# SwiGLU feed-forward: one weight load for both column parts of the down projection

## The chip, the cores and the metric

The kernel runs on one core of a Trainium2 chip (trn2). The metric is the device time of one execution in microseconds (us), lower is better. Times in the tables are medians of several executions; a profile shows one execution. In the profiles PE is the tensor engine, PEld its weight loads, DVE the vector engine, ACT the scalar engine and POOL GpSimd.

## The reference

```python
def reference(x, w_gate, w_up, w_down):      # x: 1 x 2048 x 640, bf16
    g = silu(x @ w_gate)                     # 640 x 1536
    u = x @ w_up                             # 640 x 1536
    return (g * u) @ w_down                  # 1536 x 640
```

## The kernel before

The tensor engine (PE) holds a block of 128 x 128 "weights" (the stationary operand, `lhsT`) and streams columns of the other operand (`rhs`) through it. One call of `nc.tensor.matmul` becomes two instructions: a weight load (LDWEIGHTS, engine PEld in the profile) and the matmul itself (MATMUL, engine PE). The program works on four blocks of 512 rows. In each, 24 gate and up tiles of 5 matmuls with 512 columns come first, then the down projection of four row tiles of 128 rows. The output has 640 columns, and the kernel splits each row tile into a part `po_a` of 512 columns and a part `po_b` of 128, two accumulators in PSUM, the memory that the matmuls write. Both are summed over the same twelve blocks `aT[:, kf, s0:s0+P]` as weights:

```python
for j in range(SUB):                                   # 4 row tiles in each of 4 blocks
    s0 = sb * S_BLK + j * P
    last = sb == NSB - 1 and j == SUB - 1
    po_a = psum.tile([P, DA], f32, tag="po_a", name="po_a")            # DA = 512
    for kf in range(KF):                                               # KF = 12
        nc.tensor.matmul(po_a[:], lhsT=aT[:, kf, s0 : s0 + P],
                         rhs=wd_sb[:, kf, 0:DA], start=(kf == 0), stop=(kf == KF - 1))
    po_b = psum.tile([P, D - DA], f32, tag="po_b", name="po_b")        # 128 columns
    for kf in range(KF):
        nc.tensor.matmul(po_b[:], lhsT=aT[:, kf, s0 : s0 + P],
                         rhs=wd_sb[:, kf, DA:D], start=(kf == 0), stop=(kf == KF - 1))
    ot = outp.tile([P, D], bf16)
    nc.scalar.copy(ot[:, 0:DA], po_a[:])
    # ... copy of po_b, output DMA
```

(The calls are set on fewer lines here; the loads of the inputs and the start are cut. `po_a` and `po_b` have two buffers each.) The second loop thus loads twelve weight blocks that the first loop has loaded shortly before.

## Time and profile before

| | before |
|---|---|
| time, median of the 4 runs compared with the change | 166.74 us (166.44 to 166.98) |
| span of the profiled execution | 165.2 us |
| matmuls / weight loads in the program | 907 / 907 |
| PE busy, PEld busy | 160.5 us, 80.3 us |
| matmul start to next start: 512 columns, 128 columns | 216 ns, 56 ns |
| one down projection stage (4 row tiles) | 13.04 us |

Lines of the page of the kernel before: the span, the busy times, the chain of work that ended last by engine and by line, and groups of instructions. In a group line the columns are: source line, engine, operation, out<-in, shapes, count, then busy us and mean ns of one record, then the idle time of the engine before them.

```profile
span 165.2 us, 2137 instructions
...
PE 160.5 (97%) x890; PEld 80.3 (49%) x907; DVE 34.9 (21%) x52; ACT 43.5 (26%) x81; POOL 0.7 (0%) x6
...
PE 97%; issue 1%; DVE 0%; ACT 0%
PE pg L112 31%; PE pu L112 31%; PE po_a L150 25%; PE po_b L159 7%; PE pw L98 2%; PE pt L105 1%; DVE xT L108 0%; ACT ot L173 0%
...
L150 PE MATMUL po_a<-wd_sb,aT 128*128 128x512 bf16 x185 | 43.4, 379 | 0.3
...
L150 PEld LDWEIGHTS <-aT 128*128 128x128 bf16 x192 | 18.3, 98 | 19.8
...
L159 PEld LDWEIGHTS <-aT 128*128 128x128 bf16 x192 | 12.1, 98 | 3.8
L159 PE MATMUL po_b<-wd_sb,aT 128*128 128x128 bf16 x192 | 13.3, 220 | 0.1
```

PE is busy for 97% and is 97% of the chain that ended last: no other engine or transfer holds it up. PEld is busy for 80.3 us, 30.4 us of it at the two lines of the down projection (L150 and L159). It has to be read with care, because records of PE and PEld overlap each other. A 512-column matmul is recorded with 379 ns and a 128-column matmul with 220 ns, and yet they follow each other much faster. The record of PE is incomplete too: 890 of its 907 matmuls are there, and each missing one looks like a short gap.

The timeline of the same kernel around a change from `po_a` to `po_b` (start us, duration us, then the group, merged):

```profile
start us, us, engine line op out<-in xcount [idle before <-releaser]
...
34.58 0.87 PEld L159 LDWEIGHTS <-aT 128*128 128x128 bf16 x12
34.80 0.83 PE L159 MATMUL po_b<-wd_sb,aT 128*128 128x128 bf16 x12
...
35.47 0.59 PE L150 MATMUL po_a<-wd_sb,aT 128*128 128x512 bf16 x2
```

Twelve `po_b` matmuls start at 34.80, and the next tile's `po_a` starts at 35.47: 0.67 us for twelve, 56 ns each. Twelve weight loads of about 98 ns lie in the same stretch, from 34.58 on. So the loads run beside the matmuls, also here, where the matmuls are shortest. In the single records a load starts 1 to 3 ns after the start of the matmul before it, 1 or 2 ns nearly everywhere (where it seems later, the record of a matmul is missing).

### The profile page before, as it was taken

The numbers are of one execution on the slowest core, as the hardware profiler recorded it, in microseconds if no ns is written. First come the engines' busy times: TensorE is split into PE (matmuls) and PEld (weight loads), VectorE is DVE, ScalarE is ACT, GpSimd is POOL, SyncE is SP. The second block draws the span as 40 slices with busy tenths as digits, with TensorE's granted clock in tenths as the row PEclk, the third lists the DMA queues.
The fourth block names the chain that finished last, engine by engine and source line by source line (L and its number), as shares of the span: only waits on it lengthen the run. The fifth ranks groups of instructions, "written<-read, shape, count | busy, mean of one in ns | idle before, by whom it ended". The sixth has DMA issues, their size and how long they took to land.

```text
span 165.2 us, 2137 instructions
## 1 busy us (share of the span) xinstructions
PE 160.5 (97%) x890; PEld 80.3 (49%) x907; DVE 34.9 (21%) x52; ACT 43.5 (26%) x81; POOL 0.7 (0%) x6
## 2 busy tenths in 40 slices
PE   8999999999999999999999999999999999999992
PEld 2844444455644444455554444445654444445551
DVE  0433333300013333310003333330002233331000
ACT  3042222222332222223232222222232222222222
POOL 1000000000000000000000000000000000000000
PEclk9999999999999999999999999999999999999999
DMA  5999999801110000001110000001111000000121
GB/s 147 294 326 327 362 230 223 160 29 55 40 40 0 0 4 0 0 0 42 68 55 0 0 2 0 0 4 40 40 40 40 4 0 0 0 0 0 46 78 40
DMA packets 18906, 11.27 MB, mean 68 GB/s; under 512 B 9681, under 2 KB 18897, under 8 KB 18897
## 3 DMA queue, kind: packets, MB, share of 16 engines
q1 hardware_dynamic: 18096, 10.95, 24.2%
q10 hardware_dynamic: 800, 0.20, 0.5%
q8 instruction: 7, 0.11, 0.3%
q14 instruction: 3, 0.02, 0.0%
HBM read 6.55 MB, written 2.62 MB: 56 GB/s over the span
## 4 chain that ended last, share of the span: by engine, by line
PE 97%; issue 1%; DVE 0%; ACT 0%
PE pg L112 31%; PE pu L112 31%; PE po_a L150 25%; PE po_b L159 7%; PE pw L98 2%; PE pt L105 1%; DVE xT L108 0%; ACT ot L173 0%
## 5 line engine op out<-in xcount | busy, mean ns | idle before, releaser
L112 PE MATMUL pg<-xT,wg_sb 128*128 128x512 bf16 (+2 forms) x244 | 59.5, 371 | 0.4
L112 PE MATMUL pu<-xT,wu_sb 128*128 128x512 bf16 (+2 forms) x241 | 59.6, 375 | 0.2
L141 DVE TENSOR_TENSOR aT<-sg,pu 128x512 bf16<-128x512 f32 x48 | 33.0, 687 | 109.2 <-PE pu L112 108.0
L140 ACT ACTIVATE sg<-pg 128x512 f32<-128x512 f32 x48 | 28.7, 597 | 76.2 <-PE pg L112 76.2
L150 PE MATMUL po_a<-wd_sb,aT 128*128 128x512 bf16 x185 | 43.4, 379 | 0.3
L112 PEld LDWEIGHTS <-wu_sb 128*128 128x128 bf16 x245 | 23.7, 98 | 27.9
L112 PEld LDWEIGHTS <-wg_sb 128*128 128x128 bf16 x250 | 24.0, 98 | 27.2 <-issue 0.2
L150 PEld LDWEIGHTS <-aT 128*128 128x128 bf16 x192 | 18.3, 98 | 19.8
L167 ACT CAST ot<-po_a 128x512 bf16<-128x512 f32 x16 | 9.4, 585 | 40.4 <-PE po_a L150 38.0
L159 PEld LDWEIGHTS <-aT 128*128 128x128 bf16 x192 | 12.1, 98 | 3.8
L159 PE MATMUL po_b<-wd_sb,aT 128*128 128x128 bf16 x192 | 13.3, 220 | 0.1
L98 PE MATMUL pw<-const-bfloat16-1.0 128*128 128x512 bf16 x8 | 3.6, 625 | 0.8 <-PEq L189 0.8
L169 ACT CAST ot<-po_b 128x128 bf16<-128x128 f32 x15 | 4.0, 265 | 1.1
L108 DVE COPY xT<-pt 128x640 bf16<-128x640 bf16 x4 | 2.0, 490 | 5.8 <-PE pt L105 5.7
L105 PEld LDWEIGHTS <-x_sb 128*128 128x128 bf16 x20 | 2.0, 133 | 0.6 <-DMA x_sb<-in_x_dram 0.5
L105 PE MATMUL pt<-ident,x_sb 128*128 128x128 bf16 x20 | 2.2, 289 | 0.0
L98 PEld LDWEIGHTS <-const-bfloat16-1.0 128*128 128x128 bf16 x8 | 1.0, 137 | 2.4 <-issue 2.4
L140 ACT ACT_TABLE_LOAD x1 | 1.3, 1283 | 1.3 <-PEq L189 1.3
masks.py:199 POOL TENSOR_SCALAR_AFFINE_SELECT ident<-ident 128x128 bf16<-128x128 bf16 x1 | 0.3, 292 | 0.1
L173 ACT CAST ot<-po_b 128x128 bf16<-128x128 f32 x1 | 0.3, 265 | 0.0
masks.py:197 POOL MEMSET ident<- 128x128 bf16 x1 | 0.2, 204 | 0.3 <-POOLq L189 0.3
L189 POOL MEMSET const-bfloat16-1.0<- 128x1 bf16 x1 | 0.1, 101 | 0.0
(3 smaller groups left out, 0.3 us busy)
## 6 DMA issues: line engine op xcount, KB each, us to landing
out_dram<-ot SPq DMA_DIRECT2D x15, 160.0 KB, 1.8
wd_sb<-in_w_down_dram SPq DMA_DIRECT2D x1, 1920.0 KB, 12.5
wg_sb<-in_w_gate_dram SPq DMA_DIRECT2D x3, 480.0 KB, 7.0
wu_sb<-in_w_up_dram SPq DMA_DIRECT2D x3, 480.0 KB, 7.6
x_sb<-in_x_dram SPq DMA_DIRECT2D x1, 320.0 KB, 3.2
x_sb<-in_x_dram SPq DMA_DIRECT2D x2, 160.0 KB, 3.7
wg_sb<-in_w_gate_dram SPq DMA_DIRECT2D x1, 320.0 KB, 5.0
wu_sb<-in_w_up_dram SPq DMA_DIRECT2D x1, 320.0 KB, 5.5
```

Of the source, the lines that this page charges most:

```text
L98: nc.tensor.matmul(pw[:], lhsT=ones[:, 0:P], rhs=ones, start=True, stop=True)
L105: nc.tensor.transpose(out=pt[:, kd, :], in_=x_sb[:, c, kd * P : (kd + 1) * P], identity=ident[:])
L108: nc.vector.tensor_copy(out=xT[:, :, c * P : (c + 1) * P], in_=pt[:])
L112: nc.tensor.matmul(ps[:, c0:c1], lhsT=w_sb[:, kd, fc * P : (fc + 1) * P], rhs=xT[:, kd, sb * S_BLK + c0 : sb * S_BLK + c1], start=(kd == 0 ...
L140: nc.scalar.activation(sg[:], pg[:], ACT.Silu)
L141: nc.vector.tensor_tensor(out=aT[:, fc, s_sl], in0=sg[:], in1=pu[:], op=ALU.mult)
L150: nc.tensor.matmul(po_a[:], lhsT=aT[:, kf, s0 : s0 + P], rhs=wd_sb[:, kf, 0:DA], start=(kf == 0), stop=(kf == KF - 1),)
L159: nc.tensor.matmul(po_b[:], lhsT=aT[:, kf, s0 : s0 + P], rhs=wd_sb[:, kf, DA:D], start=(kf == 0), stop=(kf == KF - 1),)
L167: nc.scalar.copy(ot[:, 0:DA], po_a[:])
L169: nc.scalar.copy(ot[:, DA:D], po_b[:])
L173: nc.scalar.copy(ot[:, DA:D], po_b[:])
L189: nc = _bacc.Bacc("TRN2", target_bir_lowering=False, num_devices=1)
```

## The change

Its intent is to load each weight block once and to stream both column parts past it. The loops are interleaved, and after compilation a pass over the instruction list deletes every weight load that loads what the engine already holds and that carries no semaphore. A semaphore is the signal by which one engine waits for another. The last row tile keeps its old order, so that the copy of `po_a` can run while `po_b` is still computed. (The diff is shortened: calls stand on one line, `down_mm` is the same matmul as a function, and the wrapper that calls `_share_weights` after `tc.compile()` is cut.)

```diff
-            for kf in range(KF):
-                nc.tensor.matmul(po_a[:], lhsT=aT[:, kf, s0 : s0 + P], rhs=wd_sb[:, kf, 0:DA], ...)
-            for kf in range(KF):
-                nc.tensor.matmul(po_b[:], lhsT=aT[:, kf, s0 : s0 + P], rhs=wd_sb[:, kf, DA:D], ...)
+            if last:
+                ...                                    # po_a, then po_b, as before
+            else:
+                for kf in range(KF):
+                    down_mm(po_a, 0, DA, kf)
+                    down_mm(po_b, DA, D, kf)
...
+def _share_weights(nc):
+    for block in nc.main_func.blocks:
+        held, drop = None, []
+        for k, ins in enumerate(block.instructions):
+            if ins.engine != mybir.EngineType.PE:
+                continue
+            if isinstance(ins, mybir.InstLdweights):
+                what = str(ins.ins[0])
+                s = ins.sync_info
+                free = s is None or not (s.on_wait or s.on_update)
+                if free and what == held:
+                    drop.append(k)
+                held = what
+        for k in reversed(drop):
+            del block.instructions[k]
```

187 loads go: 180 in the down projection (15 row tiles of 12) and 7 of the 8 of the warm-up matmuls at the start.

More of the change, by code (lines that the diff above doesn't have):

```diff
@@ L10, with _body @@
 @with_exitstack
-def kernel(
+def _body(
     ctx: ExitStack,
@@ L148, with down_mm @@
             po_a = psum.tile([P, DA], f32, tag="po_a", name="po_a")
-            for kf in range(KF):
+            po_b = psum.tile([P, D - DA], f32, tag="po_b", name="po_b")
+            def down_mm(po, d0, d1, kf):
                 nc.tensor.matmul(
-                    po_a[:],
+                    po[:],
                     lhsT=aT[:, kf, s0 : s0 + P],
-                    rhs=wd_sb[:, kf, 0:DA],
+                    rhs=wd_sb[:, kf, d0:d1],
                     start=(kf == 0),
@@ L156 @@
                 )
-            po_b = psum.tile([P, D - DA], f32, tag="po_b", name="po_b")
-            for kf in range(KF):
-                nc.tensor.matmul(
-                    po_b[:],
-                    lhsT=aT[:, kf, s0 : s0 + P],
-                    rhs=wd_sb[:, kf, DA:D],
-                    start=(kf == 0),
-                    stop=(kf == KF - 1),
-                )
+            if last:
+                for kf in range(KF):
+                    down_mm(po_a, 0, DA, kf)
+                for kf in range(KF):
+                    down_mm(po_b, DA, D, kf)
+            else:
+                for kf in range(KF):
+                    down_mm(po_a, 0, DA, kf)
+                    down_mm(po_b, DA, D, kf)
             ot = outp.tile([P, D], bf16)
@@ L174, with kernel @@
                 nc.scalar.dma_start(out=out2[s0 : s0 + P, DA:D], in_=ot[:, DA:D])
+def _share_weights(nc):
[13 more added lines that the diff above has]
+            del block.instructions[k]
+def kernel(tc, *args):
+    _body(tc, *args)
+    tc.close()
+    tc.compile()
+    _share_weights(tc.nc)
 _INS = ['x', 'w_gate', 'w_up', 'w_down']
```

## The prediction

> **What bounds the kernel now.** The tensor engine's instruction stream. The page gives PE 97% busy, and the chain of work that ended last is 97% PE (pg 31%, pu 31%, po_a 25%, po_b 7%). Matmuls are pipelined, so I read start-to-start distances in the timeline. A 128x512 matmul starts about 216 ns after its predecessor (five pg starts from 45.24 to 46.33 us). In the down projection, twelve po_b matmuls take from 41.31 to 41.98 us, 56 ns each, each behind its own weight load. The sum accounts for the span: 480 x 216 ns for gate and up, 192 x (216 + 56) ns for down, 52 us, makes 156 us; start-up (first projections at 6.0 us) and the tail (last matmul at 162 us) are the rest of 165.2 us.
>
> **What the weight loads cost now.** They are 98 ns each (groups by line), but in the timeline of single records each load starts 1 to 2 ns after the start of the matmul before it and is far enough when the next one starts. Even behind a 56 ns matmul it delays nothing: po_b to po_b is 55 to 57 ns, and po_b to the next tile's po_a, with a new load between, is 55 ns. The Trainium skill, "TensorE: Matmul & The Clock Gate", step-by-step part, says that loads are pulled ahead of matmuls in flight; this trace agrees. The same page, "Back-to-back issue gap", gives about 81 ns per 128-column matmul in a stream of load and matmul pairs, against about 56 ns without loads. By the page, dropping 180 loads would give an estimated 180 x 25 ns = 4.5 us (2.7%). The trace shows 56 ns with loads, so that gain isn't there.
>
> **What the change does.** It removes 180 of 384 loads in the down projection (all but the last tile's) and 7 of 8 in the warm-up. Matmuls, columns and evictions stay. A pair of 512 and 128 columns should cost 216 + 56 = 272 ns, as before: the load for the next pair has at least the 56 ns of the po_b matmul, which the trace shows to suffice, and changing the PSUM tile between neighbours costs nothing in this trace. Warm-up matmuls are 427 ns apart and stay so.
> Moved: po_a is complete only with po_b, so its copy (585 ns) starts about 0.6 us later in 15 tiles. Each has two buffers and a tile takes 3.26 us, so nobody waits. The last tile keeps its order, so the tail stays.
>
> **On the critical path:** 0 us, within noise. Time predicted: 166.5 us, 166.1 to 167.0. Chances: faster by over 2% 0.02, within 2% 0.96, slower by over 2% 0.02.
>
> **What would show it right.** Weight loads recorded: about 720 instead of 907, PEld busy about 68 us instead of 80.3. PE stays at 97% and po_a plus po_b in the chain at 32%. po_a to po_b 216 ns, po_b to po_a 56 ns, a tile 3.26 us. ACT's copy of po_b follows that of po_a at once. Span 165.2 us within 0.4.
>
> **What would make it wrong.** A load that starts late behind matmuls that share weights: pairs above 272 ns; 98 ns exposed in each would be 17.6 us slower. A matmul without a load of its own streaming faster than 56 ns: it would be faster, but (216 - 56)/384 columns is 0.417 ns a column, estimated from this trace, so 128 columns need 53 of the 56 ns.

## More of the kernel before

The windows view of one whole down projection stage, from its first `po_a` to the next block's first `pg` (busy us and count by engine):

```profile
core 0: us, PE busy (x) PEld busy (x) DVE busy (x) ACT busy (x) POOL busy (x), PEclk, DMA share, GB/s
32.20:45.24 13.04, 12.99 (x96) 7.37 (x96) 0.69 (x1) 2.97 (x7) 0.00 (x0) 1.00 0.11 39
```

It lasts 13.04 us. 48 pairs of 216 + 56 ns are 13.06 us: the stage is filled by the columns that stream.

## The result, and the profile after

| | before | after |
|---|---|---|
| time | 166.74 us (4 runs) | 166.91 us (166.79 to 166.94, 4 runs) |
| ratio | | 1.0007, 95% interval 0.9988 to 1.0026: the same |
| span of the profiled execution | 165.2 us | 165.0 us |
| weight loads, PEld busy | 907, 80.3 us | 720, 68.6 us |
| one down projection stage | 13.04 us | 13.04 us |

A ratio here and below is the mean time of one kernel's fast runs over that of the other's fast runs of the same rounds, so it is not quite the ratio of the quoted medians.

The lines of the page after that answer to those of before:

```profile
span 165.0 us, 1967 instructions
...
PE 161.0 (98%) x907; PEld 68.6 (42%) x720; DVE 34.8 (21%) x52; ACT 42.1 (26%) x81; POOL 0.7 (0%) x6
...
PE 97%; DVE 1%; ACT 0%; issue 0%
PE pg L112 32%; PE pu L112 31%; PE po_a L152 25%; PE po_b L152 7%; PE pw L98 2%; DVE xT L108 1%; PE pt L105 0%; ACT ot L177 0%
...
L152 PE MATMUL po_a<-wd_sb,aT 128*128 128x512 bf16 x192 | 52.0, 379 | 0.0
...
L152 PE MATMUL po_b<-wd_sb,aT 128*128 128x128 bf16 x192 | 40.3, 219 | 0.0
...
L152 PEld LDWEIGHTS <-aT 128*128 128x128 bf16 x204 | 19.5, 98 | 33.3 <-issue 31.4
```

187 weight loads and 11.7 us of PEld busy time have gone, and the span has not moved. The busy time of `po_b` seems to have grown from 13.3 to 40.3 us. Nothing got slower by that: records of 219 ns overlap their neighbours, and in the new order each `po_b` is booked alone and no longer as one of a merged run of twelve. It is a good example of a busy time that must not be read as a cost.

The timeline after, two pairs of the interleaved loop:

```profile
32.26 0.22 PE L152 MATMUL po_b<-wd_sb,aT 128*128 128x128 bf16 x1
32.26 0.10 PEld L152 LDWEIGHTS <-aT 128*128 128x128 bf16 x1 [0.33 <-issue]
...
32.31 0.38 PE L152 MATMUL po_a<-wd_sb,aT 128*128 128x512 bf16 x1
32.53 0.22 PE L152 MATMUL po_b<-wd_sb,aT 128*128 128x128 bf16 x1
32.53 0.10 PEld L152 LDWEIGHTS <-aT 128*128 128x128 bf16 x1 [0.17 <-issue]
32.59 0.38 PE L152 MATMUL po_a<-wd_sb,aT 128*128 128x512 bf16 x1
```

`po_b` starts at 32.26 and 32.53, 0.27 us apart, so a pair still takes 216 + 56 = 272 ns. There is one load in each pair, beside the `po_b` matmul. The "idle before" of 0.17 us that PEld now shows lies where the dropped load was; PE doesn't wait there.

The windows view of the stage after (columns as before):

```profile
32.04:45.08 13.04, 13.04 (x97) 4.65 (x48) 0.69 (x1) 2.26 (x6) 0.00 (x0) 1.00 0.23 64
```

13.04 us again, with 48 loads in place of 96 and 4.65 us of PEld busy in place of 7.37.

### The profile page after: what moved, and what is told of

It is laid out like the page before. It is cut to its first block, busy times and chain, and to the rows that moved or that the text cites. A ratio compares the mean times of both kernels' runs of the same rounds, so it can differ in the third digit from the quotient of the medians.

```text
span 165.0 us, 1967 instructions
## 1 busy us (share of the span) xinstructions
PE 161.0 (98%) x907; PEld 68.6 (42%) x720; DVE 34.8 (21%) x52; ACT 42.1 (26%) x81; POOL 0.7 (0%) x6
## 4 chain that ended last, share of the span: by engine, by line
PE 97%; DVE 1%; ACT 0%; issue 0%
PE pg L112 32%; PE pu L112 31%; PE po_a L152 25%; PE po_b L152 7%; PE pw L98 2%; DVE xT L108 1%; PE pt L105 0%; ACT ot L177 0%
## 5 line engine op out<-in xcount | busy, mean ns | idle before, releaser
L152 PE MATMUL po_a<-wd_sb,aT 128*128 128x512 bf16 x192 | 52.0, 379 | 0.0
L152 PE MATMUL po_b<-wd_sb,aT 128*128 128x128 bf16 x192 | 40.3, 219 | 0.0
L152 PEld LDWEIGHTS <-aT 128*128 128x128 bf16 x204 | 19.5, 98 | 33.3 <-issue 31.4
L105 PEld LDWEIGHTS <-x_sb 128*128 128x128 bf16 x20 | 1.4, 110 | 3.5 <-DMA x_sb<-in_x_dram 3.5
L98 PEld LDWEIGHTS <-const-bfloat16-1.0 128*128 128x128 bf16 x1 | 0.1, 105 | 0.7 <-issue 0.7
```

What stands on the lines that cost most here:

```text
L98: nc.tensor.matmul(pw[:], lhsT=ones[:, 0:P], rhs=ones, start=True, stop=True)
L105: nc.tensor.transpose(out=pt[:, kd, :], in_=x_sb[:, c, kd * P : (kd + 1) * P], identity=ident[:])
L152: nc.tensor.matmul(po[:], lhsT=aT[:, kf, s0 : s0 + P], rhs=wd_sb[:, kf, d0:d1], start=(kf == 0), stop=(kf == KF - 1),)
```

## The experiments

After the prediction had come true, the question was why, and whether it is general. Theory 1: a weight load runs beside the matmul in front of it, and only streamed columns count. Rivals: (A) dropping loads gains, but alternating between two PSUM tiles loses as much; (B) every load costs a little, and 187 of 907 were too few to see; (C) loads are free in any number; (D) only one load can be taken ahead; (F) only loading the same weights again is cheap. The times of the kernel before are from the same rounds. The stage lengths in the table are from the single records of each trace.

| run | time | before, same rounds | ratio (95% interval) | stage |
|---|---|---|---|---|
| interleave_own_loads | 166.82 | 166.97 | 0.9989 (0.9973 to 1.0005) | 13.04 us |
| almost_no_loads (wrong result) | 166.77 | 166.97 | 0.9998 (0.9978 to 1.0017) | 13.04 us |
| two_loads_each | 167.19 | 166.97 | 1.0018 (0.9998 to 1.0039) | 13.13 us |
| three_loads_each | 174.52 | 166.68 | 1.0464 (1.0440 to 1.0488) | 14.96 us |
| pieces64_own_loads | 170.15 | 166.97 | 1.0196 (1.0179 to 1.0213) | 13.84 us |
| pieces64_shared | 169.95 | 166.82 | 1.0190 (1.0163 to 1.0217) | 13.84 us |
| pieces64_distinct_loads | 172.28 | 166.68 | 1.0328 (1.0304 to 1.0351) | 14.35 us |
| pieces32_own_loads | 206.49 | 166.68 | 1.2377 (1.2350 to 1.2405) | 22.79 to 23.09 us |
| pieces32_shared | 203.30 | 166.68 | 1.2189 (1.2165 to 1.2213) | 22.18 us |

### The new order with all loads kept

```diff
 # against the changed kernel
     tc.compile()
-    _share_weights(tc.nc)
+    pass
```

> The changed order (po_a, po_b alternate) with all 907 loads kept. Theory 1 (a load runs beside the matmul before it, and only the columns count): ratio to the kernel before 1.000, within 0.3%; pairs 272 ns. Rival A (dropping the loads gains, and alternating between two PSUM tiles costs as much, so that both cancel): slower by what the drop gains, by the page's 25 ns a load an estimated 4.5 us, ratio about 1.027.

Measured: 166.82 us, ratio 0.9989. (The 25 ns a load of the expectation are the difference of the page's 81 and 56 ns in the prediction.) The timeline:

```profile
32.15 0.64 PEld L152 LDWEIGHTS <-aT 128*128 128x128 bf16 x5
...
32.42 0.38 PE L152 MATMUL po_a<-wd_sb,aT 128*128 128x512 bf16 x1
32.63 0.22 PE L152 MATMUL po_b<-wd_sb,aT 128*128 128x128 bf16 x1
32.69 0.38 PE L152 MATMUL po_a<-wd_sb,aT 128*128 128x512 bf16 x1
```

Every matmul has its load again (five in a row in the PEld line), and the pairs are 0.27 us apart (32.42 to 32.69), as without the second load. Rival A is out: the new order costs nothing by itself, so there is no hidden gain that it cancels.

### Nearly no loads at all

```diff
 # against the changed kernel, with the loops of po_a and po_b in their old order
-                if free and what == held:
+                if free and k > 0 and held is not None:
```

This deletes every load that carries no wait. The result is wrong (relative error 7.04). It is the limit of anything that sharing loads could ever give.

> Order of the kernel before; every weight load that carries no wait is dropped, so some 25 of 907 stay. Wrong result on purpose. It is the upper bound for whatever dropping loads can gain. Theory 1: ratio 1.000 within 0.5%; matmul starts stay 216 and 56 ns apart. Rival B (each load costs a little and 187 of 907 were too few to see): even 2 ns a load would show as 1.8 us, ratio 0.989 or lower.

Measured: 166.77 us, ratio 0.9998. Of the page the busy times; then the timeline of PE around one `po_b` run, as shown of before.

```profile
PE 159.7 (97%) x890; PEld 2.2 (1%) x22; DVE 34.9 (21%) x52; ACT 43.6 (26%) x81; POOL 0.7 (0%) x6
```

The timeline (start us, duration us, group):

```profile
34.30 0.83 PE L152 MATMUL po_b<-wd_sb,aT 128*128 128x128 bf16 x12
34.97 1.24 PE L152 MATMUL po_a<-wd_sb,aT 128*128 128x512 bf16 x5
```

22 loads and 2.2 us of PEld are left, and twelve `po_b` matmuls still take from 34.30 to 34.97, 0.67 us. Rival B is out. A cost of 2 ns for each load would have been 1.8 us; the interval ends at 0.2% or 0.4 us. The 885 loads that are gone, of 907, cost nothing that the runs can see.

### Two loads in front of each matmul

```diff
 # against the kernel before, in both loops of the down projection
             for kf in range(KF):
+                nc.tensor.ldweights(aT[:, kf, s0 : s0 + P])
                 nc.tensor.matmul(
```

> Order of the kernel before, every matmul of the down projection gets a second, identical weight load in front (384 more). Theory 1: behind a 216 ns matmul two loads of about 56 ns still fit, so po_a stays at 216 ns; behind a 56 ns matmul they don't, so po_b goes to about 112 ns each, 192 x 56 ns = 10.8 us slower, ratio about 1.065. Rival C (loads are free whatever their number): ratio 1.000. Rival D (only one load can be taken ahead, the second waits for the matmul in flight): po_a also slower by 50 to 100 ns each, 20 to 30 us in all.

Measured: 167.19 us, ratio 1.0018. This is a miss of theory 1 in the form that it had: I had taken the 56 ns between the loads of `po_b` for what a load needs, so two should have made 112 ns. They made 58 ns. The timeline (each load is a record of its own here; the later ones of the same kind are left out):

```profile
34.66 0.85 PE L161 MATMUL po_b<-wd_sb,aT 128*128 128x128 bf16 x12
34.66 0.10 PEld L160 LDWEIGHTS <-aT 128*128 128x128 bf16 x1
34.70 0.10 PEld L161 LDWEIGHTS <-aT 128*128 128x128 bf16 x1
34.72 0.10 PEld L160 LDWEIGHTS <-aT 128*128 128x128 bf16 x1
...
35.35 0.38 PE L151 MATMUL po_a<-wd_sb,aT 128*128 128x512 bf16 x1
```

The twelve `po_b` matmuls take from 34.66 to 35.35, 0.69 us in place of 0.67. In the single records the second load of a pair starts 42 ns after the first, and the matmul 13 ns after the second. Rival D is out too: `po_a` stays at 216 ns. Rival C, free in any number, survived this run.

### Pieces of 64 columns, each with its own load

```diff
 # against the changed kernel
-    _share_weights(tc.nc)
+    pass
...
-                    down_mm(po_a, 0, DA, kf)
-                    down_mm(po_b, DA, D, kf)
+                    for p in whole:                          # po_a, po_b
+                        for q in [p] if kf in (0, KF - 1) else cut(*p):   # 64 columns each
+                            piece(*q, kf)
```

The first and the last `kf` stay whole, so that one matmul opens and one closes each sum in PSUM, as before.

> Changed order; in 10 of 12 kf of each row tile the 640 columns are cut into ten matmuls of 64, each with its own load. At 0.417 ns a column plus 2.5 ns (estimated from the 216 and 56 ns of before) 64 columns stream in 29 ns. Theory 1 with a load interval of about 56 ns: ten at 56 ns instead of 272 ns, 160 x 288 ns = 46 us slower. Rival C (loads hide behind any matmul): ten at 29 ns, 160 x 20 ns = 3 us slower.

Measured: 170.15 us, 3.2 us slower. Theory 1 with a load of 56 ns had said 46 us, the hidden loads 3 us. In the timeline ten matmuls with ten loads repeat every 0.29 us (32.95 to 33.24), so 29 ns each:

```profile
32.92 0.77 PEld L168 LDWEIGHTS <-aT 128*128 128x128 bf16 x24
32.95 0.40 PE L168 MATMUL po_a<-wd_sb,aT 128*128 128x64 bf16 x8
33.19 0.22 PE L168 MATMUL po_b<-wd_sb,aT 128*128 128x64 bf16 x2
33.24 0.40 PE L168 MATMUL po_a<-wd_sb,aT 128*128 128x64 bf16 x8
```

So a load needs no more than 29 ns of the matmul in front of it. Theory 1 got a second form: a load costs only if the matmul in front of it is shorter than what the load needs, which is at most 29 ns.

### Other weights in each load

```diff
 # against the run before: kf is the inner loop again
-                for kf in range(KF):
-                    for p in parts:
-                        for q in ...: piece(*q, kf)
+            for p in whole:
+                for q in cut(*p):
+                    for kf in range(KF):
+                        piece(*q, kf)
```

> The down projection in 64-column pieces, each piece running through its 12 kf before the next, so that every matmul's load brings other weights than the one before (1920 loads). Theory 1, second form (a load that stands behind a matmul needs no more than 29 ns of it, whatever it holds): starts 29 ns apart as in the run with ten equal loads, 192 x 20 ns = 3.8 us slower, ratio about 1.023. Rival F (loading the weights that are already there is cheap, and only that was shown; other weights take up to the 56 ns that the kernel before has): up to 192 x 288 ns = 55 us slower.

Measured: 172.28 us, ratio 1.0328. Here the first and the last `kf` are cut into pieces too. The starts are 29 ns apart over nearly all of the 1920 matmuls, so rival F, by which I would have seen up to 55 us, is out. By the ratio the run is 5.5 us slower than before, 1.7 us more than the 3.8 us that I expected. The waits view (who waited for whom, us in total, times, longest us) names the most of it; the same four stalls appear once for the load and once for its matmul:

```profile
PEld L168 <- DVE aT L141: 1.2, 4, 0.3
...
PE po_a L168 <- DVE aT L141: 0.7, 4, 0.2
```

The twelfth `kf` of a block's first piece comes too soon. In the trace it doesn't even come twelfth: the compiled order puts eleven matmuls of `po_b` and one more of `po_a` in front of it. But those 23 starts take only 0.67 us. In the first block VectorE writes the last part of `aT` until 33.20 us, and the load that waits for it starts at 33.26, where 32.89 + 0.03 would have been its turn. In the single records the start is 374 ns after the one before it in place of 29 ns, once in each of the four blocks: 1.4 us together.

### Three loads in front of each matmul

```diff
 # against the kernel before
             for kf in range(KF):
+                nc.tensor.ldweights(aT[:, kf, s0 : s0 + P])
+                nc.tensor.ldweights(aT[:, kf, s0 : s0 + P])
                 nc.tensor.matmul(
```

> Order of the kernel before, three loads in front of every matmul of the down projection. In the run with two, the second load started 42 ns after the first, the matmul 13 ns after the second, and the next load 2 to 3 ns after the matmul: 58 ns in all against 56. Theory 1, second form: with three, 42 + 42 + 13 + 2 = 100 ns for a po_b matmul, po_a stays at 216 to 218 ns: 192 x 44 ns = 8.4 us slower, ratio about 1.05. Rival C (loads never cost): ratio 1.00, po_b at 56 to 58 ns.

Measured: 174.52 us, ratio 1.0464; expected were 8.4 us or about 1.05, measured 7.8 us. The timeline (later loads left out):

```profile
34.57 1.28 PE L163 MATMUL po_b<-wd_sb,aT 128*128 128x128 bf16 x12
34.58 0.10 PEld L161 LDWEIGHTS <-aT 128*128 128x128 bf16 x1
34.62 0.10 PEld L162 LDWEIGHTS <-aT 128*128 128x128 bf16 x1
34.66 0.10 PEld L163 LDWEIGHTS <-aT 128*128 128x128 bf16 x1
...
35.72 0.60 PE L152 MATMUL po_a<-wd_sb,aT 128*128 128x512 bf16 x2
```

The twelve `po_b` matmuls take from 34.57 to 35.72, 1.15 us in place of 0.67: 97 ns each. Rival C is out: a load is not free in any number. Loads in a row, with no matmul between them, come about 40 ns apart (34.58, 34.62, 34.66), and the third no longer fits beside a matmul of 56 ns. Beside the 216 ns of `po_a` it does, and there nearly all starts stay 216 ns apart. Why loads in a row need 40 ns each, when loads with a matmul between them came 29 ns apart, no run shows.

### Pieces of 64 under one load

The edit is that of the pieces with own loads, but the deletion pass is kept.

> The pieces of 64 under one load per kf. With own loads they start 29 ns apart, which is what 64 columns need by the estimate of 0.417 ns a column plus 2.5 ns. Theory 1, second form: sharing gains nothing here either, 29 ns apart, time equal to the run with own loads (170.2 us, ratio 1.02 to the kernel before) within 0.4%. If the loads cost anything at this size, faster than that run by 1664 - 204 = 1460 loads x their cost: 1 ns each would be 1.5 us.

Measured: 169.95 us, ratio 1.0190 against 1.0196 with 1460 more loads in the down projection. The timeline has the same 0.29 us for ten matmuls (32.99 to 33.28):

```profile
32.99 0.40 PE L168 MATMUL po_a<-wd_sb,aT 128*128 128x64 bf16 x8
33.23 0.22 PE L168 MATMUL po_b<-wd_sb,aT 128*128 128x64 bf16 x2
...
33.28 0.40 PE L168 MATMUL po_a<-wd_sb,aT 128*128 128x64 bf16 x8
```

Sharing gains nothing measurable at 64 columns either: both stages last 13.84 us.

### Pieces of 32, with own loads and under one load

> As the run with pieces of 64, with twenty pieces of 32 in 10 of 12 kf, each with its own load. By columns alone 32 x 0.417 + 2.5 = 16 ns each, 160 x 48 ns = 8 us slower than before. By the skill's page on TensorE a matmul start never comes less than 25 ns after another: 160 x (500 - 272) ns = 36 us slower. Theory 1, second form: if a pair of load and matmul needs more than that, 28 ns or so, 160 x (560 - 272) = 46 us, and here first the loads would cost something.

> The same pieces of 32 under one load per kf, the change's own rewrite. Theory 1, second form: at the floor of the matmuls alone, 16 to 25 ns each (8 to 36 us slower than before), and faster than the run with own loads only if that one shows starts further apart. It tells from which matmul size on sharing a load can gain at all.

Measured: 206.49 and 203.30 us, 39.8 and 36.6 us slower than before. The timeline with own loads:

```profile
34.21 0.55 PE L168 MATMUL po_a<-wd_sb,aT 128*128 128x32 bf16 x16
34.61 0.25 PE L168 MATMUL po_b<-wd_sb,aT 128*128 128x32 bf16 x4
```

Sixteen starts take 0.40 us, 25 ns each, and so do nearly all starts in both traces, not the 16 ns that the columns would need. The Trainium skill, "TensorE: Matmul & The Clock Gate", section "Wait — 56ns, not 53.3ns?", says that a start never comes less than about 25 ns after another: 160 x (500 - 272) ns = 36 us, an estimate from that figure, and 36.6 us measured with shared loads. So a load still fits within the shortest distance that any run here shows between two matmuls, and the 28 ns that theory 1 allowed for are not needed. Most of these loads bring weights that are already there, but not all: at each of the 135 changes of `kf` from one cut `kf` to the next, the load brings other weights behind a matmul of 32 columns, and there too the next start comes after 25 ns.

Sharing does gain 3.2 us here. It is no cost of each load, as the groups show. With own loads:

```profile
L168 PEld LDWEIGHTS <-aT 128*128 128x128 bf16 x3264 | 85.9, 96 | 6.5 <-issue 2.1
L168 PE MATMUL po_a<-wd_sb,aT 128*128 128x32 bf16 (+1 forms) x2576 | 85.6, 177 | 1.6 <-issue 1.6
```

The same groups with shared loads:

```profile
L168 PE MATMUL po_a<-wd_sb,aT 128*128 128x32 bf16 (+1 forms) x2576 | 84.2, 177 | 0.0
...
L168 PEld LDWEIGHTS <-aT 128*128 128x128 bf16 x204 | 19.5, 96 | 70.0 <-issue 67.6
```

With own loads PE sat idle before `po_a` for 1.6 us, put down to "issue", which means that it waited for nothing that the profile shows; with shared loads it didn't. In the single records there are six such places, with starts 343 to 553 ns apart in place of 25, together 2.5 us; five more of 88 to 135 ns bring it to 2.9 us. This program has 3067 more PE instructions, and in the list of transfers its instruction queue moved 29 packets against 17. It may be that instructions arrive too slowly at two for every 25 ns. The trace's single packets fit this: in the down projection they start mostly 3.4 to 4.6 us apart (with shared loads 6.1 to 7.4 us), and each of the eleven stalls ends 1.0 to 1.5 us after a packet has landed. That is a coincidence in time in one trace; no run tells it from another cause, so it stays open.

## Why the prediction was right

Point by point:

- What bounds the kernel. Right: streamed columns do. The down stage lasts 13.04 us before, after, in the new order with all loads, and with nearly no loads.
- Loads hide behind the matmul in front of them. Right for this kernel: that they cost nothing is shown by `almost_no_loads` (0.9998) rather than argued. The Trainium skill, "TensorE: Matmul & The Clock Gate", section "Step-by-step: what each phase is for", says that the engine pulls loads ahead of matmuls in flight, and this trace agrees: loads start 1 to 3 ns after the start of the matmul in front.
- The 4.5 us that the page's 81 ns for a load and matmul pair of 128 columns would have promised. Rightly refused: the pair took 56 ns in the trace, 56 ns without the load, and the gain is absent.
- No cost of the alternation. Right: 0.9989 for the order alone.
- Signs. 720 loads were recorded (predicted about 720), PEld was busy for 68.6 us (about 68), the chain has 25% + 7% for the down projection (32%), pairs take 272 ns, the span is 165.0 us. The copy of `po_a` starts 3.40 us after the start of the stage in place of 2.79 us, 0.6 us later as predicted, and nobody waits for it.
- The time. Predicted were 166.5 us (166.1 to 167.0), measured 166.91. The band is about as wide as the spread of one kernel (the kernel before took 166.44 to 167.32 us in all its runs), so that the median fell inside it is partly luck; the unchanged stage of 13.04 us is not.

What was wrong was a reading of mine after the prediction, in the first expectations: the distance of 56 ns between loads in the trace before was the distance of the matmuls, which set the pace, and not what a load needs. It took runs with more loads to see that.

For the size of the kernel: 2 x 3 x 2048 x 640 x 1536 = 12.08 GFLOP in 166.74 us are 72.4 TFLOP/s. By the peak of 78.6 TFLOP/s that the Trainium skill states (the table at the head of "TensorE: Matmul & The Clock Gate") this is an estimated 92%. No experiment pointed to a version faster than both kernels.

## What to carry to other kernels

Before you drop weight loads, read the distance between matmul starts with and without loads in front, not the busy time of PEld: if the distance already fits the columns (here 216 ns for 512 and 56 ns for 128), the loads are hidden and their removal is worth nothing. Then test the limit first: one kernel without nearly all loads, with a wrong result, tells at once what any sharing could give at most. A busy time, or a distance that other instructions set, is only an upper bound of an instruction's own cost; to learn that cost, make more of it until it shows.

## What the Trainium skill lacked or had wrong

- "TensorE: Matmul & The Clock Gate", "Back-to-back issue gap": it gives about 81 ns (128 columns) and 131 ns (512 columns) for each matmul in a stream of load and matmul pairs. The runs show 56 and 216 ns, with loads and without; the figures that it gives for matmuls alone (55.6 and 215.7 ns) fit the pairs too.
- The same page, Part 3, "What overlaps and what doesn't": it says that a load overlaps matmuls in flight only where the row groups differ. Here every load fills all 128 rows, and it starts 1 to 3 ns after the start of the matmul in front of it, which is recorded with 220 or 379 ns. Part 2 of the page, which allows for a background weight buffer, fits.
- The same page gives the duration of a load, but lacks how much of a matmul a load needs: one load fits even in the distance of 25 ns, the shortest seen here; with two loads in a row a matmul of 56 ns takes 58 ns, with three 97 ns; loads in a row (of the same weights, in these runs) come about 40 ns apart.
- "Perfetto Trace Analysis", "Identifying the Most-Contended Engine", and "Trainium Kernel Development and Optimization", "Performance Expectations": they call the busy share of LDWEIGHTS a good measure of the distance to the roofline. Summed over the single records, as the first of them says, it was 1%, 43%, 54% and 76% of the span in kernels of 166.8 (nearly no loads, wrong result), 166.9 (after), 166.7 (before) and 167.2 us (two loads each), so it measures nothing of the kind here. (PEld busy on the pages, which counts overlapping loads once, is 1%, 42%, 49% and 53%.) The share of peak FLOP/s, which the same sentence names, is an estimated 92% in all of them, as their times are the same.
